# Top-32 attention and a PReLU feed-forward on one core: score products moved behind h, VectorE's order fixed, the norm after the searches, and half of the wide copies on VectorE

## The chip, the cores and the metric

The kernel runs on one core of one Trainium2 chip. The metric is the device time of one execution in microseconds (us); lower is better. The kernel before takes 896.75 us, the median of three runs (896.16 to 897.48).

A core has five engines with queues of their own: PE (TensorE, matrix products; its weight loads are listed as PEld), ACT (ScalarE), DVE (VectorE), POOL (GpSimd) and SP (SyncE, which here only issues DMAs). Each works through its own list in order and waits where an instruction needs what another engine has yet to deliver.

## What is computed

Eight batches of eight heads, 576 queries and keys each, head size 64. Of each row of scores only those that are not below the 32nd largest are kept; the heads' outputs, side by side, are the 4608 tokens of a feed-forward layer (512 to 2048 to 512) with a PReLU between.

```python
scores = scale * q @ k.T                     # per head, 576 x 576
kth = np.partition(scores, -32, axis=-1)[..., -32:-31]
attn = softmax(np.where(scores >= kth, scores, -1e9))
x = concat_heads(attn @ v)                   # 4608 x 512
h = x @ w_in                                 # 4608 x 2048
g = np.maximum(h, 0) + alpha * np.minimum(h, 0)
out = g @ w_out                              # 4608 x 512
```

## The kernel before, in words

**Duos and slots.** The work on the 64 heads is cut into 144 *duos*: a duo is two blocks of 128 query rows of one pair of heads, or (a *tail duo*, `"m"`) the last 64 rows of the heads of two pairs. Each batch has 18 duos, two of them tail duos. The kernel is one loop, written out at build time, of 148 *slots* (`for n in range(ND + 4)`), and in slot n several duos stand at different stages: n is searched, n+1 is copied out, n-2 is compared and its rows searched (`count`, `row`), n-4 is masked (`relu`), n-5 is exponentiated (`exp`), n-6 is multiplied with v (`av`), and the pair of duos that ended with n-7 is normalised in even slots (`norm`).

**The stages of a duo.** `st_qk`: PE writes the scores, 128 x 2 x 576 in fp32, into `ps_sc`, a tile of three PSUM banks that exists once. `st_exit`: ACT copies it to SBUF (`s_sb`, six buffers). `dve_slot`: VectorE takes the 8 largest of each of six groups of 96 columns per row (12 MAX8, which write `up` and `small`); in an odd slot, for both duos of the pair n-1, n, it folds these to a threshold (`bot`, `th`, `neg`, `n8`, and in `turn` the first column of `p`). `st_count`: ACT takes the sign of (threshold - score) with a sum (`sg`, `cs`). `st_y`: GpSimd multiplies scores by that sign (`y`). `row`: VectorE finds the 8 largest of each row of `y`, one row search (0 or 1) for each of the duo's two blocks. `pick_steps` (`eq_`, `pk_`, `kt_`): three small VectorE steps choose the exact 32nd value (`KT`). `st_relu`: ACT makes a mask (`r`), and GpSimd subtracts it from the scores. `st_exp`: ACT writes exp to `w`, and SP issues a transposing DMA to `wT`. `st_av`: PE multiplies with v into `xo`, one PSUM buffer for a pair of duos; 10 products, 20 in a tail duo. `norm_a`, `norm_b`: VectorE's reciprocal of the sums, and the product `x` (`xm` for tails), which frees `xo`; SP then transposes x to `xT`.

**The feed-forward part** is fed in between. `h_pe` issues the 8 products (16 for 128-token chunks) of one unit of h (`ph`), `h_dve` is VectorE's ReLU to `gT`, `o_pe` issues a quarter of an output tile (`pz`), `o_act` is ACT's copy to `o_sb`. `keep_warm` issues four idle products (`rest`) where there is no h or no pz.

**Preparation.** `prep_pe` transposes k and q of a head pair for a later batch by PE (`tps`): two units of width 512 and one narrow unit per pair. `prep_evac` copies them to `qkT`; the list `pend` is emptied at the end of the slot, and `on_dve` decides between VectorE and ACT: wide ones by VectorE before slot 17 and by ACT from then on, narrow ones by VectorE after slot 16. `ph`, `tps` and `rest` share two PSUM buffers (`ps_h`).

**What sets the order.** Every engine is wrapped in `Ordered`, whose calls keep program order (line 31, which is why nearly every row of the profile has L31). An exception are the VectorE steps that go through `sm`: they use columns of one PSUM tile, `small`, and `declare_no_dep` takes the order among them away but for true overlaps, so the scheduler may move them, and with them the searches between. In the built list of before, the first search of the next slot stands ahead of `turn` and of the last row search, and `eq_` stands in the odd slot ahead of the fold.

PE's list in a slot of before is: h(n) or idle products, pz if ready, transposes, score(n+2), attention (n-6), and pz or idle products. ACT's list is: two signs, exp, two masks, the score copy of n+1, then output and `qkT` copies. GpSimd's is: two products `y`, two subtractions, and a cast of v in most slots.

## Time and profile before

| | |
|---|---|
| median of three runs | 896.75 us |
| the profiled execution | 892.84 us, of which 891.1 us from the first to the last instruction (the span) |
| mean granted PE clock | 0.967 of full speed |
| score copies: first, 25th, 144th | at 9.6, 152.7 and 834.0 us |
| PE, VectorE, ACT, GpSimd busy | 752.6, 745.7, 774.9, 757.3 us |

A row of a group reads: line, engine, operation, output <- input (buffer numbers left out), shapes, x count, then busy time in us and the mean ns of one, then the idle time of the engine just before these instructions and what ended it. A row of the waits reads: engine and what it wanted to do <- engine and what it waited for: us in total, times, longest. A row of the timeline reads: start, length, engine, line, operation, output <- input, shapes, count, and in brackets the idle time before it. Operations of one engine overlap a little at their ends, so the distance of two starts can be shorter than the length given.

### The profile page before, as it was taken

The page shows a single profiled execution, that of the slowest core. Times are in us where ns is not written, and L with a number is a line of the kernel's source. Part 1 is how long each engine was busy: PE and PEld are TensorE (multiplying, and loading weights), DVE is VectorE, ACT ScalarE, POOL GpSimd, SP SyncE. Part 2 cuts the span into 40 slices and gives each one's busy share as a digit, 9 for nine tenths or more (in the row PEclk, how much of TensorE's full clock was granted, in tenths as well). Part 3 has the DMA queues.
Part 4 walks back from the last instruction along what each step waited for, and adds up shares of the span by engine and source line. Part 5 has one row for each costly group of instructions (what it writes and reads, how often), then busy time and mean ns, then how long its engine had stood idle before and what let it go on. Part 6 is the DMA issues. An engine that isn't in the chain of part 4 may idle for free.

```text
span 891.1 us, 17698 instructions
## 1 busy us (share of the span) xinstructions
PE 752.6 (84%) x5299; PEld 431.9 (48%) x5386; DVE 745.7 (84%) x3451; ACT 774.9 (87%) x1279; POOL 757.3 (85%) x708
## 2 busy tenths in 40 slices
PE   8785989888888888888888888888878898888887
PEld 5342444444545454455445454454544555445554
DVE  4999786898997989998988889989898878898842
ACT  4899787899999999999998999999999879998930
POOL 2899787888998999989998899989998878998950
PEclk9899997999999999999989999999999989999999
DMA  8698974355555545555545556555555554343351
GB/s 177 160 199 149 158 126 86 78 108 114 125 112 113 119 96 125 103 121 114 123 100 111 108 101 134 101 125 114 116 112 119 102 103 92 79 89 63 85 101 40
DMA packets 344167, 100.19 MB, mean 112 GB/s; under 512 B 338032, under 2 KB 338048, under 8 KB 344064
## 3 DMA queue, kind: packets, MB, share of 16 engines
q1 hardware_dynamic: 340992, 91.87, 51.0%
q0 software_dynamic: 1872, 6.82, 3.2%
q8 instruction: 44, 0.72, 0.3%
q14 instruction: 59, 0.48, 0.2%
q10 hardware_dynamic: 1200, 0.30, 0.2%
HBM read 36.71 MB, written 9.44 MB: 52 GB/s over the span
## 4 chain that ended last, share of the span: by engine, by line
ACT 30%; PE 28%; DVE 13%; issue 12%; POOL 8%; DMA 6%; SPq 1%; ACTq 0%; POOLq 0%
PE ps_sc L31 9%; ACT r L31 9%; ACT sg L31 9%; ACT s_sb L31 7%; PE ph L31 6%; PE pz L31 5%; PE xo L31 5%; POOL y L31 5%; DVE p L31 4%; ACT w L31 3%; POOL s_sb L31 3%; DMA wT<-w 3%; DVE small L31 3%; DVE gT L31 3%; DMA q_st<-in_q_dram 3%
## 5 line engine op out<-in xcount | busy, mean ns | idle before, releaser
L31 POOL TENSOR_TENSOR y<-s_sb,sg 128x576 f32<-128x576 f32 x288 | 362.3, 1279 | 95.4 <-ACT sg L31 93.5
L31 POOL TENSOR_TENSOR s_sb<-s_sb,r 128x576 f32<-128x576 f32 x288 | 362.1, 1278 | 6.1 <-ACT r L31 6.0
L31 PE MATMUL ps_sc<-qkT 64*128 64x512 f32 (+2 forms) x768 | 184.2, 576 | 110.1 <-ACT s_sb L31 109.4
L31 ACT ACTIVATE sg<-s_sb,p 128x576 bf16<-128x576 f32 x288 | 220.8, 769 | 53.2 <-DVE p L31 53.1
L31 DVE MAX8 up<-s_sb 128x8 f32<-128x96 f32 x864 | 211.3, 245 | 15.5 <-ACT s_sb L31 14.3
L31 DVE MAX8 p<-y 128x8 f32<-128x576 f32 x288 | 210.4, 750 | 3.9 <-POOL y L31 3.8
L31 DVE MAX8 small<-s_sb 128x8 f32<-128x96 f32 x864 | 211.9, 252 | 0.0
L31 ACT ACTIVATE r<-s_sb,KZ 128x576 bf16<-128x576 f32 x288 | 205.5, 762 | 5.7 <-DVE KZ L31 5.6
L31 ACT ACTIVATE w<-s_sb 128x1152 bf16<-128x1152 f32 x144 | 165.7, 1151 | 4.7 <-POOL s_sb L31 4.7
L31 DVE TENSOR_SCALAR gT<-ph 128x512 bf16<-128x512 f32 x144 | 99.0, 688 | 76.9 <-PE ph L31 76.8
L31 ACT COPY s_sb<-ps_sc 128x1152 f32<-128x1152 f32 x144 | 158.2, 1099 | 3.2 <-PE ps_sc L31 3.0
L31 PE MATMUL ph<-xT,w_in_b 128*128 128x256 bf16 (+1 forms) x1408 | 153.0, 257 | 0.1
L31 PE MATMUL pz<-w_out_b,gT 128*128 128x512 bf16 x546 | 145.4, 386 | 5.2 <-issue 3.1
L31 PEld LDWEIGHTS ps_sc<-qkT 64*128 64x128 f32 (+1 forms) x768 | 54.1, 170 | 168.8 <-ACT s_sb L31 143.0
L31 PE MATMUL xo<-v,wT 128*128 128x65 bf16 (+3 forms) x1600 | 128.4, 200 | 7.3 <-DMA wT<-w 7.3
L31 PEld LDWEIGHTS <-w_in_b 128*128 128x128 bf16 x1408 | 116.6, 99 | 32.3 <-issue 3.0
L31 PEld LDWEIGHTS <-wT 128*128 128x128 bf16 (+3 forms) x1600 | 98.7, 100 | 38.0 <-DMA wT<-w 8.6
L31 PEld LDWEIGHTS ps_sc<-kd,qkT 128*128 128x128 f32 x256 | 38.9, 192 | 99.2 <-issue 98.5
L31 PEld LDWEIGHTS <-gT 128*128 128x128 bf16 x576 | 57.2, 99 | 57.8 <-issue 6.8
L31 PE MATMUL ps_sc<-kd,qkT 128*128 128x128 f32 x256 | 63.8, 332 | 0.0
L31 PE MATMUL rest<-idle 128*128 128x512 bf16 x209 | 59.2, 402 | 2.1 <-DVE qkT L31 0.7
L31 ACT ACTIVATION_READ_ACCUMULATOR sg<-s_sb,p 128x1 f32 x288 | 54.6, 190 | 0.0
(57 smaller groups left out, 562.5 us busy)
## 6 DMA issues: line engine op xcount, KB each, us to landing
k_st<-in_k_dram SPq DMA_DIRECT2D x64, 128.0 KB, 2.8
v_st<-in_v_dram SPq DMA_DIRECT2D x64, 128.0 KB, 2.7
q_st<-in_q_dram SPq DMA_DIRECT2D x62, 128.0 KB, 2.8
out_dram<-o_sb SPq DMA_DIRECT2D x31, 256.0 KB, 2.4
w_st<-in_moe_w_out_dram POOLq DMA_DIRECT2D x4, 1024.0 KB, 6.2
wT<-w SPq DMA_TRANSPOSE x144, 3.5
w_in_b<-in_moe_w_in_dram POOLq DMA_DIRECT2D x4, 512.0 KB, 5.8
k_st<-in_k_dram SPq DMA_DIRECT2D x32, 32.0 KB, 2.5
```

The source lines that it names most:

```text
L31: return self.tc.keep_in_program_order(f(*a, **kw))
```

## The change

Four things are changed.

1. In the loop, `st_qk(n + 1)` is called right after `h_pe` (or the idle products) at the head of slot n, from slot 1 on, and the call of `st_qk(n + 2)` between the transposes and the attention products goes. PE's list becomes: h(n) or idle products, score(n+1), pz, transposes, attention (n-6), pz or idle products.
2. `Ordered` records each call. A step named in `small` is placed behind the last step that isn't (`anchor`), and the next one that isn't is placed behind all small ones since. VectorE's built list is then the program's: `turn` and the last row search stand ahead of the next slot's first search, and `eq_` stands in the even slot after the first search of `small`.
3. In even slots `norm_a` is called after `h_dve`, and `norm_b` between the row searches 0 and 1. Before, the reciprocal stood after the first six searches and x after the twelfth, both ahead of gT.
4. Wide `qkT` copies go to VectorE in even slots after slot 16 too. These are 24 of them, in slots 22 to 124; on ACT 24 fewer stand in the built list. They stand at the end of VectorE's even slot.

The lists of GpSimd and SP keep their order.

```diff
--- before.py
+++ after.py
@@ -23,14 +23,38 @@
 
     def __init__(self, tc, eng):
         self.tc, self.eng = tc, eng
+        self.anchor, self.loose, self.last, self.small = None, [], None, set()
 
     def __getattr__(self, name):
         f = getattr(self.eng, name)
 
         def call(*a, **kw):
-            return self.tc.keep_in_program_order(f(*a, **kw))
+            ins = self.tc.keep_in_program_order(f(*a, **kw))
+            self.settle()
+            self.last = ins.ins
+            return ins
 
         return call
+
+    def behind(self, ins, other):
+        self.tc.add_manual_dep(
+            ins, other.name,
+            mybir.DependencyInfo(mybir.DependencyClass.NoSync, mybir.DependencyReason.DATA),
+            reason="program order")
+
+    def settle(self):
+
+        if self.last is None:
+            return
+        if self.last.name in self.small:
+            if self.anchor is not None:
+                self.behind(self.last, self.anchor)
+            self.loose.append(self.last)
+        else:
+            for i in self.loose:
+                self.behind(self.last, i)
+            self.anchor, self.loose = self.last, []
+        self.last = None
 
 
 def fast_path(tc, q, k, v, moe_w_in, moe_w_out, moe_alpha, out, flag):
@@ -123,6 +147,7 @@
                     if hit(writes, r[1]) or hit(writes, r[2]) or hit(reads, r[2])]
             tc.declare_no_dep(ins.ins, group="small", keep=keep, reason="other columns")
             tc.add_to_no_dep_group("small", ins.ins)
+            DVE.small.add(ins.ins.name)
             recent.append((ins.ins, reads, writes))
             del recent[:-60]
 
@@ -305,14 +330,15 @@
                             sm(m, [], [(o, o + 8)])
                             if picks:
                                 picks.pop(0)()
-                    if norm and i == 0:
-                        norm_a(norm)
-                if norm:
-                    norm_b(norm)
                 if n % 2 == 0:
                     h_dve()
+                    if norm:
+                        norm_a(norm)
                     for d in rows:
                         row(d, 0)
+                    if norm:
+                        norm_b(norm)
+                    for d in rows:
                         row(d, 1)
                 else:
                     fold, negate, least, turn = threshold_steps(n // 2)
@@ -701,6 +727,8 @@
                     st_av(m)
             if not h_pe() and not end:
                 keep_warm()
+            if n and on(n + 1):
+                st_qk(n + 1)
             late = len(hq) > (9 if n < 118 else 4) and n % 2 == 0 or end
 
             for m in duos_at("count", n):
@@ -720,8 +748,6 @@
             run(n, "cast")
             run(n, "lin_out")
             run(n, "prep", 2 if n < 4 else 1)
-            if on(n + 2):
-                st_qk(n + 2)
             if not end:
                 for m in duos_at("av", n):
                     st_av(m)
@@ -737,7 +763,8 @@
                 late_o[0] = 0
             while pend:
                 short = len(pend[0][0].shape) == 3
-                on_dve = short and n > 16 or pend[0][0].shape[1] == 512 and n < 17
+                wide = pend[0][0].shape[1] == 512
+                on_dve = short and n > 16 or wide and (n < 17 or n % 2 == 0)
                 prep_evac(DVE.tensor_copy if on_dve else ACT.copy)
             if n == 1:
                 sm(DVE.tensor_copy(alpha_ps, aps), [], [(304, 320)])
```

## Prediction

> **What bounds the kernel now.** I read the page first (span, busy shares), then the busy time by stretch, then the waits of the long middle stretch, then that stretch's timeline engine by engine. The page:

> ```profile
> span 891.1 us, 17698 instructions
> ...
> PE 752.6 (84%) x5299; PEld 431.9 (48%) x5386; DVE 745.7 (84%) x3451; ACT 774.9 (87%) x1279; POOL 757.3 (85%) x708
> ```

> Four engines have nearly the same work, and none is full: an even load that loses time in handing over. The table of stretches (start:end, length, then busy time of PE, PEld, DVE, ACT, POOL, then granted clock) says where:

> ```profile
> 0.00:152.00 152.00, 122.92 (x682) 63.02 (x694) 119.37 (x559) 123.86 (x211) 116.95 (x136) 0.92 0.78 151
> 152.00:834.00 682.00, 585.66 (x4190) 339.61 (x4257) 602.17 (x2828) 628.58 (x1035) 616.84 (x553) 0.98 0.51 107
> ```

> The middle stretch runs from the score copy of duo 24 to that of duo 143: 119 slots, 682/119 = 5.73 us each, 11.46 a pair of slots. ACT is busy for 628.6 of it and waits for the rest. The waits of that stretch name the ring:

> ```profile
> PE ps_sc L31 <- ACT s_sb L31: 89.8, 81, 2.5
> POOL y L31 <- ACT sg L31: 63.3, 69, 4.1
> DVE gT L31 <- PE ph L31: 60.0, 82, 3.9
> ACT sg L31 <- DVE p L31: 47.3, 36, 4.4
> ```

> Read as a ring: PE waits for ACT's copy out of the one score tile, VectorE waits for PE's h, ACT waits for VectorE's threshold, GpSimd waits for ACT's sign. One turn of it, slots 70 and 71 of the timeline, in fences for ACT, PE, VectorE (DVE) and GpSimd (POOL) (start, length, engine, group, idle before it):

> ```profile
> 417.84 0.78 ACT L31 ACTIVATE sg<-s_sb,p 128x576 bf16<-128x576 f32 x1 [1.44 <-DVE p L31]
> ...
> 419.37 1.15 ACT L31 ACTIVATE w<-s_sb 128x1152 bf16<-128x1152 f32 x1
> ...
> 421.76 1.10 ACT L31 COPY s_sb<-ps_sc 128x1152 f32<-128x1152 f32 x1
> 422.76 0.58 ACT L31 COPY qkT<-tps 128x512 f32<-128x512 f32 x1
> 423.23 0.78 ACT L31 ACTIVATE sg<-s_sb,p 128x576 bf16<-128x576 f32 x1
> ...
> 429.13 0.77 ACT L31 ACTIVATE sg<-s_sb,p 128x576 bf16<-128x576 f32 x1
> ```

> ```profile
> 416.46 1.13 PE L31 MATMUL ps_sc<-qkT 64*128 64x512 f32 x4 [0.83 <-ACT s_sb L31]
> ...
> 417.93 1.62 PE L31 MATMUL xo<-v,wT 128*64 128x65 bf16 x20
> 419.71 1.03 PE L31 MATMUL pz<-w_out_b,gT 128*128 128x512 bf16 x4 [0.16 <-issue]
> 420.57 1.04 PE L31 MATMUL ph<-xT,w_in_b 128*128 128x256 bf16 x8
> 421.45 0.60 PE L31 MATMUL tps<-ident_f,k_st 128*128 128x128 f32 x4
> 422.91 1.13 PE L31 MATMUL ps_sc<-qkT 64*128 64x512 f32 x4 [0.86 <-ACT s_sb L31]
> ...
> 424.29 0.78 PE L31 MATMUL xo<-v,wT 128*128 128x65 bf16 x10
> ...
> 429.69 0.78 PE L31 MATMUL xo<-v,wT 128*128 128x65 bf16 x10
> ```

> ```profile
> 418.86 0.18 DVE L31 SCALAR_TENSOR_TENSOR pk<-small,p 128x36 f32<-128x36 f32 x1
> 418.96 0.25 DVE L31 MAX8 up<-s_sb 128x8 f32<-128x96 f32 x1
> ...
> 420.63 0.41 DVE L31 TENSOR_TENSOR xm<-xo,KZ 128x256 bf16<-128x256 f32 x1
> 421.65 0.69 DVE L31 TENSOR_SCALAR gT<-ph 128x512 bf16<-128x512 f32 x1 [0.61 <-PE ph L31]
> 422.25 1.41 DVE L31 MAX8 p<-y 128x8 f32<-128x576 f32 x2
> 423.58 0.24 DVE L31 MAX8 up<-s_sb 128x8 f32<-128x96 f32 x1
> ...
> 425.50 0.18 DVE L31 TENSOR_TENSOR small<-small,cs 128x36 f32<-128x36 f32 x1
> ...
> 426.95 0.69 DVE L31 TENSOR_SCALAR gT<-ph 128x512 bf16<-128x512 f32 x1 [0.55 <-PE ph L31]
> ...
> 428.79 0.24 DVE L31 MAX8 up<-s_sb 128x8 f32<-128x96 f32 x1
> 428.95 0.15 DVE L31 TENSOR_SCALAR p<-small 128x4 f32<-128x4 f32 x1
> ```

> ```profile
> 418.78 2.52 POOL L31 TENSOR_TENSOR y<-s_sb,sg 128x576 f32<-128x576 f32 x2 [1.20 <-ACT sg L31]
> ```

> PE's score product (416.46) starts when ACT has emptied the tile; the attention products, pz and h stand behind it, so h ends at 421.45 and VectorE's gT stands idle for 0.61, and for 0.55 in the next slot. VectorE then runs through to the threshold at 428.95, and at 429.13 ACT's sign follows it. The pair took 429.13 - 417.84 = 11.29. From the score copy's end to the threshold the path is product 1.5, attention 0.75 (1.6 in a tail duo), pz 1.0, h 0.9, and then VectorE.

> **The change part by part.**

> *Score product behind h.* No instruction is added; PE's order turns to h(n), score(n+1), pz, transposes, attention. h(n) no longer stands behind the wait for ACT, so it is ready before VectorE wants it: the 60.0 of gT waits and the 47.3 of ACT waits lose their cause. What is late next is the score tile itself. On time, score(n+1) takes 1.5 from the copy's end (422.91 to 424.3), and ACT copies that tile again 421.76 - 417.84 = 3.9 after its slot begins: 2.4 us of slack for PE. In front of it stands h, whose PSUM buffer comes free with a gT of the slot before, or with a transposed tile's copy; I cost that at nothing as long as the 2.4 hold. The transposes and wT's DMA are met one slot earlier: w ends at 420.5, its transposing DMA takes 3.5 (below), so wT is there at 424.0 and is used at 429.7, 5.7 later. Afterwards it is used behind the score product of 422.91, at 424.3 plus pz or transposes: 0.3 to 1.8 of margin while PE is on time, more when it is late.

> ```profile
> wT<-w SPq DMA_TRANSPOSE x144, 3.5
> ```

> *VectorE's order pinned.* The threshold (428.95) no longer has the next slot's first search (428.79, 0.16 earlier) before it, nor the small compare (425.50, about 0.1) in its slot, which moves to the even slot. The ring to ACT is 0.26 shorter; VectorE's sum is unchanged. The early search cost no wait here, and it can't any more.

> *Norm behind the searches.* The reciprocal comes behind gT, and x (0.41) behind the first row search. By distances of starts 12 searches take 1.92 (423.58 to 425.50), a small step 0.1 (418.86 to 418.96), gT 0.6 and a row search 0.67 (422.25 to 423.58 for two). So x ends later. In an even slot, from its first search: searches 1.92, four small steps 0.4, gT 0.6, row 0.67, x 0.41: 4.0, against 1.92 + 0.4 + 0.41 = 2.75 now. PE's next attention product waits for x, since xo has one buffer. Queued behind it: pz, h(n+1), score(n+2). From x: 0.75 + 1.0 + 0.9 + 1.45 = 4.1, so score(n+2) ends 8.1 after VectorE's slot began. ACT's slot begins at the threshold, a row search (0.67) before VectorE's; its next slot begins 4.92 later (417.84 to 422.76, without copies) and wants the tile 3.9 after that: 4.92 + 3.9 - 0.67 = 8.15. Just in time; 0.8 late after a tail duo. xT's DMA starts 1.3 later too, but its h comes two slots later, which covers it.

> *Half of the wide copies to VectorE.* 24 copies, slots 22 to 124:

> ```profile
> L31 ACT COPY qkT<-tps 128x512 f32<-128x512 f32 x52 | 30.2, 581 | 7.4 <-PE tps L31 7.4
> L31 DVE COPY qkT<-tps 128x512 f32<-128x512 f32 x12 | 8.0, 681 | 12.0 <-PE tps L31 12.0
> ```

> ACT loses 24 x 0.58 = 13.9 of busy time, 24 x 0.47 = 11.3 by the distance of starts (422.76 to 423.23); I take 11.5, near the lower one, since ACT's groups follow each other by starts. VectorE gains 24 x 0.68 = 16.3, or 14.4 at 0.6, a gT's distance; I take 14.6 for the same reason and keep both ends for the range. The copy stands at the even slot's end, where VectorE is ahead of ACT's score copy by about 0.4; beyond that it is on the path.

> *Sum, middle stretch.* ACT 628.6 - 11.5 = 617; VectorE 602.2 + 14.6 = 617; GpSimd 616.8 as before; PE 586. No engine can make it in under 617, 65 below now. Three engines at the same floor won't meet it: by pairs, VectorE's mean pair is 602.2/59.5 = 10.1, with a wide copy 10.7; GpSimd's is 616.8/59.5 = 10.4; ACT's is 9.84, with a wide copy left to it 10.3, with an output copy too 10.8. Of 18 slots, four pairs have wide copies (10.75, the dearest engine), four have the narrow one (10.4), one has none (10.1): 94.7. The score tile that comes 0.8 late behind each of two tail duos adds 0 to 1.5, transposed tiles that ACT waits for about as much; I add 1.6: 96.3, or 5.35 a slot, 637 for 119. That is 45 less than 682.

> *First stretch.* 152 stays within about 4 either way. For: 5.0 us of ACT's waits for the threshold lie there. Against: a stall at 88.5,

> ```profile
> 88.54 1.06 PE L31 MATMUL xo<-v,wT 128*128 128x65 bf16 x10 [4.51 <-DMA wT<-w]
> ```

> will now stand in front of a score product that today is already issued; its copy comes some 7 us later, most of which is lost today to a VectorE copy behind the same stall. I take -1. *Drain:* same order of pz and h, no saving, +1 for work left over.

> The profiled execution took 892.84 (891.1 span and 1.7 around it), 3.9 under the median 896.75 of the runs. 45 off the median: **852**.

> **The rivals.**

> *A, the wait moves into PE's ring through x.* x to x: attention 0.75, pz 1.0, h 0.9, score 1.45, pz 1.0, transposes 0.5, attention 0.75, pz 1.0, h 0.9 = 8.25, then gT, reciprocal, row, x 1.78: 10.0 a pair, 11.4 with a tail duo (20 products for 10, and 0.6 more of scores). For it: PE's own work, 586/59.5 = 9.85 a pair, leaves little. Against: many slots lack one pz. If ACT waits add up to 11.1 a pair, 59.5 x 11.1 = 660: 22 off, 875.

> *B, slower: the wait for x cools PE.* After an idle of 2.05 us, the next stretch ran at half clock (stretch, length, PE busy, clock):

> ```profile
> 443.50:445.50 2.00, 0.15 (x1) 1.00 0.50 96
> 445.50:447.00 1.50, 1.30 (x6) 1.00 0.51 96
> 447.00:449.00 2.00, 2.00 (x17) 0.54 0.00 0
> ```

> On time, PE would reach the even slot's attention product up to 2 us before x (score tile taken up 1 us before VectorE's slot begins, then 1.5 + 1.0 + 0.5, against 4.0). If each even slot held such a gap, A's 8.25 would be stretched: 8.25/c + 1.78 passes today's 11.46 where the mean clock of the middle stretch falls under c = 0.85 (0.98 now). At 0.8 the pair is 12.1, 720 for the stretch: +38, 935. Against: PE's work of 9.85 in 10.7 leaves 0.85 of idle a pair, so once it runs late the gap is short. [...]

> *C, the reordering does nothing.* Should the threshold still end ACT's waits (GpSimd's rows late instead of h), only ACT's copies are saved: 11.5, less the 0.6 a time on VectorE, which then is in the ring: 885 to 897, I take 890.

> *D, floor reached.* All waits go: 65 off, 832.

> **How the numbers follow.** Forecast (838 to 868) 0.62; A 0.16; B 0.09; C 0.07 (0.04 of it faster, 0.03 no change); D 0.06. Faster is then 0.62 + 0.16 + 0.04 + 0.06. Low end: 834, since the floor itself is reached at most by D. High end: A with both dear copy costs, 882. Left out: B, most of C, a bit of D, 0.2 in all. The runs before differ by 0.15%, so 0.2% is about what can be told from no change. Faster 0.88, same 0.03, slower 0.09.

> **What will show it.** Right: in the middle stretch, gT's wait for h from 60 to under 15, ACT's wait for p from 47 to under 20, ACT and GpSimd over 95% busy, slots of 5.35; ACT 24 wide copies fewer. A: a new wait of PE's attention products (or their weight loads) for VectorE's x, and ACT's score copy waiting for PE, over 20 us. B: a mean clock under 0.85 there. C: ACT's wait for p still above 40 with gT no longer waiting. The forecast is wrong in size if the wait of attention for wT, which no row of the middle stretch's longer waits shows today, passes some 10 us, or if the first stretch grows past 158.

## Result, and the profile after

The changed kernel takes 883.02 us (median of four runs, 880.58 to 885.65) against 896.62 for the kernel before: a ratio of 0.985, 95% interval 0.982 to 0.988. It is faster, as forecast, but by 13.6 us (1.5%) instead of 45, and 1 us above the range's high end of 882. The profiled execution took 883.55, its span is 881.3. In all ratios, executions more than 1.5% longer than the fastest of the same kernel are left out; the one profiled of copies_back was such a one, so only its other times are used.

The page of the changed kernel, span and engines:

```profile
span 881.3 us, 17690 instructions
...
PE 773.3 (88%) x5299; PEld 438.1 (50%) x5386; DVE 764.1 (87%) x3475; ACT 765.5 (87%) x1255; POOL 755.6 (86%) x708
```

ACT's work fell by 9.4 and VectorE's rose by 18.4, near the forecast. PE's rose by 20.7 with the same number of products. The stretches, cut at the 25th and the last score copy (161.9 and 822.0 now; columns as before):

```profile
0.00:162.00 162.00, 126.11 (x698) 64.06 (x710) 123.41 (x562) 124.26 (x212) 118.33 (x137) 0.91 0.70 142
162.00:822.00 660.00, 601.07 (x4172) 343.71 (x4238) 616.49 (x2849) 618.88 (x1010) 613.80 (x552) 0.95 0.55 110
822.00:881.30 59.30, 46.09 (x433) 30.33 (x440) 24.17 (x66) 22.34 (x36) 23.43 (x21) 0.93 0.32 74
```

The middle stretch is 660.1 long from copy to copy: 21 shorter, where 45 was forecast. The first is 9 longer (forecast -1), the last 2 longer (forecast +1). The waits of the middle stretch answer to the four rows shown of before, with the new ones between:

```profile
POOL y L32 <- ACT sg L32: 45.5, 52, 3.2
PE xo L32 <- DVE x L32: 43.3, 31, 2.8
ACT s_sb L32 <- PE ps_sc L32: 34.1, 25, 3.3
DVE gT L32 <- PE ph L32: 19.7, 22, 2.4
...
PE pz L32 <- ACT o_sb L32: 6.6, 8, 1.1
...
ACT sg L32 <- DVE p L32: 4.3, 10, 0.5
```

The old ring is gone: ACT's wait for the threshold fell from 47.3 to 4.3, VectorE's for h from 60.0 to 19.7, and PE no longer waits for ACT's score copy (89.8 before). In their place stands a new ring: PE waits 43 us for x, and ACT 34 us for the score tile. One turn of it, one of the longest, with PE, VectorE and ACT of the changed kernel (start, length, idle before); the score product in it is a tail duo's, which has 16 pieces:

```profile
461.58 0.22 PE L32 MATMUL tps<-ident_f,q_st 64*128 64x64 f32 x1
464.25 1.04 PE L32 MATMUL xo<-v,wT 128*128 128x65 bf16 x10 [2.44 <-DVE x L32]
465.22 0.61 PE L32 MATMUL pz<-w_lin_b,xT 128*128 128x512 bf16 x1
465.62 1.91 PE L32 MATMUL pz<-w_out_b,gT 128*128 128x512 bf16 x4
467.33 1.91 PE L32 MATMUL ph<-xT,w_in_b 128*128 128x128 bf16 x16
469.17 2.84 PE L32 MATMUL ps_sc<-qkT 64*64 64x512 f32 x16
```

```profile
463.70 0.40 DVE L32 TENSOR_TENSOR x<-xo,KZ 128x256 bf16<-128x256 f32 x1
...
469.28 0.69 DVE L32 TENSOR_SCALAR gT<-ph 128x512 bf16<-128x512 f32 x1 [1.59 <-PE ph L32]
...
473.27 0.26 DVE L32 MAX8 up<-s_sb 128x8 f32<-128x96 f32 x1 [1.19 <-ACT s_sb L32]
```

```profile
467.58 1.43 ACT L32 ACTIVATE r<-s_sb,KZ 128x576 bf16<-128x576 f32 x2
472.12 1.12 ACT L32 COPY s_sb<-ps_sc 128x1152 f32<-128x1152 f32 x1 [3.11 <-PE ps_sc L32]
```

PE is early at 461.8 and stands until x is written at 464.1. Then everything that is queued behind has to run first: attention, pz, h, and only then the score product that ACT would have taken at 469.0. It comes at 472.1. The pieces are also longer than usual (pz 1.91 for 1.03, h 1.91 for 1.06 at 459.01). The stretch table of PE shows why (stretch, length, PE busy, clock, then DMA share and GB/s):

```profile
460.00:462.00 2.00, 1.80 (x10) 1.00 0.62 137
462.00:464.00 2.00, 0.00 (x0) 0.94 0.24 48
464.00:466.00 2.00, 1.75 (x12) 0.50 0.96 180
466.00:468.00 2.00, 2.00 (x11) 0.50 0.35 70
468.00:470.00 2.00, 2.00 (x14) 0.50 0.53 155
470.00:472.00 2.00, 2.00 (x16) 0.86 0.82 153
```

The half clock began within the idle time, at 463.75, and lasted until 470.58. The mean over the middle stretch went from 0.98 to 0.95.

Two turns of the changed kernel with the same idle time show what the clock makes of it. Both times PE waited 2.17 us for x ahead of a tail duo's attention, and what stood behind was of about the same length: an output quarter or idle products, h, and an ordinary score product. PE's row and ACT's next score copy of each:

```profile
211.95 1.59 PE L32 MATMUL xo<-v,wT 128*64 128x65 bf16 x20 [2.17 <-DVE x L32]
...
312.23 1.64 PE L32 MATMUL xo<-v,wT 128*64 128x65 bf16 x20 [2.17 <-DVE x L32]
```

```profile
217.17 1.12 ACT L32 COPY s_sb<-ps_sc 128x1152 f32<-128x1152 f32 x1 [0.36 <-PE ps_sc L32]
...
318.82 1.12 ACT L32 COPY s_sb<-ps_sc 128x1152 f32<-128x1152 f32 x1 [1.73 <-PE ps_sc L32]
```

Behind the first the clock stayed at 1.00 and the score product ended 5.1 us after PE had x; behind the second it was 0.50 from 313.6 to 317.0, and the same took 6.5 us. It is so in the whole middle stretch: 14 of ACT's 25 waits for the score tile, 27.5 of the 34.1 us, end within a half-clock stretch or at most 6 us behind one, though these stretches with the 6 us behind them cover only 139 of the 660 us.

### The profile page after: what moved, and what is told of

The parts are those of the page before. It is cut to its first block, busy times and chain, and to the rows that moved or that the text cites. A ratio compares the mean times of both kernels' runs of the same rounds, so it can differ in the third digit from the quotient of the medians.

```text
span 881.3 us, 17690 instructions
## 1 busy us (share of the span) xinstructions
PE 773.3 (88%) x5299; PEld 438.1 (50%) x5386; DVE 764.1 (87%) x3475; ACT 765.5 (87%) x1255; POOL 755.6 (86%) x708
## 4 chain that ended last, share of the span: by engine, by line
PE 36%; DVE 29%; ACT 14%; POOL 10%; issue 5%; DMA 4%; SPq 1%; ACTq 0%; POOLq 0%
PE ps_sc L32 10%; PE pz L32 10%; DVE small L32 9%; DVE p L32 7%; PE ph L32 7%; DVE up L32 5%; PE xo L32 5%; POOL s_sb L32 5%; POOL y L32 4%; ACT sg L32 4%; ACT s_sb L32 4%; DVE gT L32 3%; PE rest L32 3%; ACT r L32 3%; ACT w L32 2%
## 5 line engine op out<-in xcount | busy, mean ns | idle before, releaser
L32 DVE MAX8 up<-s_sb 128x8 f32<-128x96 f32 x864 | 212.6, 246 | 18.9 <-ACT s_sb L32 18.4
L32 DVE MAX8 p<-y 128x8 f32<-128x576 f32 x288 | 215.2, 747 | 10.2 <-POOL y L32 9.7
L32 DVE MAX8 small<-s_sb 128x8 f32<-128x96 f32 x864 | 216.6, 251 | 0.0
L32 PE MATMUL ps_sc<-qkT 64*128 64x512 f32 (+2 forms) x768 | 186.1, 583 | 3.5 <-ACT s_sb L32 3.5
L32 PE MATMUL xo<-v,wT 128*128 128x65 bf16 (+3 forms) x1600 | 129.0, 201 | 67.7 <-DVE x L32 47.1
L32 PE MATMUL ph<-xT,w_in_b 128*128 128x256 bf16 (+1 forms) x1408 | 161.4, 265 | 0.9 <-PE xo L32 0.5
L32 PE MATMUL pz<-w_out_b,gT 128*128 128x512 bf16 x557 | 152.3, 396 | 5.6 <-issue 3.2
L32 PEld LDWEIGHTS <-w_in_b 128*128 128x128 bf16 x1408 | 121.5, 103 | 38.0 <-issue 9.5
L32 PE MATMUL rest<-idle 128*128 128x512 bf16 x209 | 62.7, 421 | 4.7 <-DVE qkT L32 2.7
```

The costliest lines, as they stand in the source:

```text
L32: ins = self.tc.keep_in_program_order(f(*a, **kw))
```

## The experiments

The table gives medians and ratios to the kernel before (with 95% intervals), and from each profile the middle stretch (score copy 25 to 144), its clock, and the three waits of the ring there in us ("-": not among the longest waits of that stretch). The profiled execution can lie some us off the median: that of no_idle took 856.9, that of head_old 879.9, that of score_only 879.9.

| kernel | us | ratio | middle, us | clock | PE for x | PE for output copy | ACT for score tile |
|---|---|---|---|---|---|---|---|
| before | 896.6 | 1 | 681.2 | 0.98 | - | - | - |
| changed | 883.0 | 0.985 (0.982 to 0.988) | 660.1 | 0.95 | 43.3 | 6.6 | 34.1 |
| norm_back | 873.7 | 0.977 (0.973 to 0.981) | 646.9 | 0.97 | 14.2 | 24.6 | 22.6 |
| norm_last | 901.4 | 1.006 (1.002 to 1.010) | 672.5 | 0.95 | 46.8 | 4.6 | 47.1 |
| pz_first | 894.3 | 0.995 (0.991 to 0.998) | 670.3 | 0.95 | 15.2 | 41.7 | 45.0 |
| skip_only | 877.8 | 0.979 (0.976 to 0.982) | 652.1 | 0.97 | 36.6 | - | 30.1 |
| pz_first_skip | 856.1 | 0.959 (0.953 to 0.964) | 629.6 | 0.99 | 12.6 | - | 11.2 |
| norm_back_skip | 851.6 | 0.953 (0.948 to 0.958) | 626.8 | 0.99 | 12.6 | - | 7.6 |
| no_idle | 851.4 | 0.948 (0.944 to 0.953) | 629.5 | 0.96 | 26.6 | - | 10.7 |
| score_only | 883.6 | 0.988 (0.983 to 0.993) | 660.0 | 0.97 | 8.8 | 37.7 | 21.8 |
| copies_back | 881.1 | 0.983 (0.980 to 0.987) | not used | | | | |
| free_order | 881.5 | 0.983 (0.979 to 0.986) | 660.1 | 0.96 | 41.5 | 9.2 | 31.6 |
| head_old | 875.5 | 0.978 (0.974 to 0.983) | 663.4 | 0.95 | 44.0 | 6.7 | 34.0 |
| v3 | 851.8 | 0.950 (0.947 to 0.954) | 629.7 | 0.99 | 13.4 | - | 7.6 |
| after_no_idle | 880.7 | 0.982 (0.976 to 0.988) | 659.2 | 0.95 | 53.4 | 9.9 | 33.5 |
| skip_no_idle | 872.3 | 0.972 (0.966 to 0.977) | 646.1 | 0.96 | 55.6 | - | 25.9 |

### x early and x later: norm_back and norm_last

norm_back takes one edit of the four back; norm_last goes further the other way.

```diff
# norm_back: against the changed kernel, in the searches and after them
+                    if norm and i == 0:
+                        norm_a(norm)
+                if norm:
+                    norm_b(norm)
                 if n % 2 == 0:
                     h_dve()
-                    if norm:
-                        norm_a(norm)
                     for d in rows:
                         row(d, 0)
-                    if norm:
-                        norm_b(norm)
-                    for d in rows:
                         row(d, 1)
# norm_last: norm_b(norm) behind row(d, 1) instead of behind row(d, 0)
```

> The changed kernel with the norm back among the searches (the reciprocal after six searches, x after twelve); the other three edits stay. Theory G (the gap): in even slots PE waits up to 2.8 us for x, its clock halves, and the score product behind runs late, 34 us of ACT's waits in the middle stretch. x some 1.3 us earlier shortens each gap below the 2 us that halve the clock: ACT's wait for the score tile in the middle stretch falls from 34 to under 12, the clock there rises from 0.95 to 0.98, and the time falls by 15 to 25, to about 863. Theory F (the floor): three engines with 614 to 619 of work each can't do better than the 660 of the middle stretch by any move of x; the time stays within 4 of 883. Theory O (the old order of the norm was there for a reason): the reciprocal waits for PE's attention inside the searches, so VectorE loses 10 or more and the time is over 890.

> The changed kernel with x behind both row searches of the even slot, 0.67 us later than now: a larger dose of the suspected wait. Theory G: PE's wait for x in the middle stretch goes from 43 to 65 to 85, more gaps pass 2 us, the clock falls to 0.93 or less and ACT's wait for the score tile rises from 34 to 45 to 60: 893 to 908. Theory F: within 5 of 883.

x earlier by 1.3 us gains 9 us, x later by 0.67 loses 18 (12 in the middle stretch, 8 in the first, 2 won back in the last), so x's place is a cause, with a dose. Theory G's way to norm_last's time was right only in part: ACT's wait for the score tile rose to 47.1 as expected, but PE's wait for x came to 46.8, not 65 to 85, and the clock stayed at 0.95. The 2 us of theory G is the author's estimate, from the gap of 2.05 us in the trace of before, behind which the clock was 0.50; no run shows a limit there (last section).

norm_back's gain is smaller than theory G expected (873.7, not 863; ACT's wait 22.6, not under 12); theories F and O, with times within 4 of 883 or over 890, fall. Its profile shows what holds the gain back: a wait that was 6.6 in the changed kernel. The row from norm_back's waits in its middle stretch, and one such place on PE:

```profile
PE pz L32 <- ACT o_sb L32: 24.6, 19, 2.2
```

```profile
577.08 0.78 PE L32 MATMUL xo<-v,wT 128*128 128x65 bf16 x10
579.89 0.38 PE L32 MATMUL pz<-w_lin_b,xT 128*128 128x512 bf16 x1 [2.03 <-ACT o_sb L32]
580.11 1.02 PE L32 MATMUL pz<-w_out_b,gT 128*128 128x512 bf16 x4
580.97 1.04 PE L32 MATMUL ph<-xT,w_in_b 128*128 128x256 bf16 x8
581.94 1.13 PE L32 MATMUL ps_sc<-qkT 64*128 64x512 f32 x4
```

The output quarter at the slot's end (`o_pe` after `o_act`) is the first of a new tile and needs the one output tile, which ACT copies out only after its score copy, at the end of its slot. Before the change the score product stood ahead of it and had waited for that same slot end, so the quarter found the tile free: no such wait is among those of before. With the score product at the slot's head, PE is there most of a slot earlier, and h and the next score product stand behind the wait.

### The gap filled, and the output tile: pz_first, norm_back_skip, pz_first_skip, skip_only

```diff
# skip (norm_back_skip, pz_first_skip, skip_only)
+                held = len(stores)
                 o_act()
+                freed = n > 24 and not end and len(stores) < held
...
-                if not (end or ready() > 2) or not o_pe():
+                if not (end or ready() > 2) or freed or not o_pe():
# pz_first (pz_first, pz_first_skip): in even slots after 26 the attention
# products come behind this output quarter or the idle products
+            swap = n > 26 and n % 2 == 0
-            if not end:
+            if not end and not swap:
                 for m in duos_at("av", n):
                     st_av(m)
...
                 late_o[0] = 0
+            if not end and swap:
+                for m in duos_at("av", n):
+                    st_av(m)
```

> The changed kernel, but from slot 28 on the last output quarter (or the idle products) of an even slot is put ahead of the attention products that wait for x, so that PE has 1.0 us of work in the gap; x stays late. Theory G: gaps of 2.0 to 2.8 become 1.0 to 1.8, the clock stays up (0.97 or more in the middle stretch), ACT's wait for the score tile falls from 34 to under 15, the time by 12 to 22, to about 866. Theory F: within 4 of 883. A theory that the wait itself, not the clock, costs the time also expects a gain, but one without a rise of the clock.

> The kernel with the norm back among the searches, and in a slot in which ACT's output copy is issued, from slot 25 on, idle products stand in place of the output quarter at the slot's end. Theory P (that quarter needs the one output tile, which ACT frees only at the end of its slot, and h and the score product stand behind it: 24.6 us of PE's waits in 19 places): PE's wait for the output copy falls under 6, ACT's wait for the score tile from 22.6 to under 10, the middle stretch from 647 to 635 to 640, the time from 873.7 to about 864. Rival F (the floor of three engines is what is left, the wait is hidden): within 3 of 873.7.

> The changed kernel (x late) with both: the output quarter of even slots ahead of attention, and none in a slot in which ACT's output copy is issued. Theories G and P together: the first kernel of this kind lost to the output tile (41.7 us of PE's waits for the copy) what it gained in the gap; without that, the gap ahead of attention is filled, the clock in the middle stretch is 0.97 or more, ACT waits under 20 for the score tile, and the time is 865 to 874. If the gap and the clock didn't matter, the time stays with the changed kernel's, 880 to 886.

> The changed kernel with one edit: in a slot in which ACT's output copy is issued, from slot 25 on, no output quarter stands at the slot's end, but idle products. x stays late, behind the first row search. Theory P2 (the late output quarter and the late x are two waits in one ring, each of which is dear because the other has used up PE's slack): without the quarter most of the loss goes although x stays, 858 to 868, with a clock of 0.97 or more in the middle stretch. Theory G alone (the wait for x is the cause): the quarter waited for only 6.6 us in the changed kernel, so 876 to 883, and the wait for x stays over 35.

pz_first missed both ways, at 894.3 where 866 or about 883 was expected: filling the gap with the output quarter only put that quarter's own wait (41.7) into it. With the quarter gone where the tile isn't free, the same filling gives 856.1 (865 to 874 was expected), though x is as late as in the changed kernel. norm_back_skip takes 851.6, 12 less than theory P expected, a ratio of 0.953 (0.948 to 0.958) to the kernel before and some 31 under the changed one; of all kernels only no_idle and v3, which are built on it, are level with it.

The two waits don't add: x alone is worth 9 (883.0 to 873.7), the quarter alone 5 (877.8), both 31. That they don't add is measured; why is not shown. Theory P2 explains it so: a wait is dear when the other has used up PE's slack. But P2 also expected 858 to 868 of skip_only, which took 877.8 with 36.6 us of waits for x, as theory G alone said, so the two waits aren't alike: x has to come early, or its gap be filled, before putting off the quarter pays.

The page of norm_back_skip and the waits of its middle stretch show what such a kernel looks like when the ring is open:

```profile
span 848.1 us, 17855 instructions
...
PE 770.6 (91%) x5376; PEld 435.5 (51%) x5466; DVE 759.9 (90%) x3475; ACT 763.3 (90%) x1255; POOL 754.3 (89%) x706
```

```profile
POOL y L32 <- ACT sg L32: 12.7, 23, 1.3
PE xo L32 <- DVE x L32: 12.6, 16, 1.7
...
ACT s_sb L32 <- PE ps_sc L32: 7.6, 12, 1.1
```

Its middle stretch is 626.8 with 616.6 of ACT's work in it. So the floor of 617 in the prediction's sum stands, and was met within 10 us.

### Is it the half clock? no_idle, after_no_idle, skip_no_idle

```diff
         def keep_warm():
+            if now[0] > 24:
+                return
```

> The best kernel so far (norm among the searches, no output quarter behind an output copy; 851.6) without idle products from slot 25 on: PE has some 30 groups of four fewer, 25 to 30 us of work, and no wait is added. Theory G in its strict form (the price of a gap is the half clock behind it): gaps that the idle products filled pass 2 us, the clock in the middle stretch falls from 0.99 to 0.96 or less, and the time rises by 6 to 20, to 858 to 872. Rival W (a gap costs only its own length): less work for PE, so the time is the same or lower, 846 to 853.

> The changed kernel without idle products from slot 25 on: x late, the output quarters where they are. PE has about 14 groups of idle products fewer there, some 12 to 15 us of work. Theory K (in the changed kernel, where PE has no time to spare, the half clock behind a gap is the price): the clock in the middle stretch falls below 0.95 and the time rises by 5 to 15, to 888 to 898. Theory W (PE's lost time is the price, whatever it comes from; the clock costs only what it adds to PE's work): less work, so 875 to 885.

> The changed kernel without an output quarter behind an output copy (877.8) and without idle products from slot 25 on, 25 to 30 us of PE work less; x stays late. Theory K: the clock falls from 0.97 to 0.94 or less and the time rises to 882 to 895. Theory W: 866 to 878, and the wait for x grows by about what the work shrinks.

Three kernels, each without the idle products from slot 25 on. The clock of the middle stretch fell in two of them (0.99 to 0.96, 0.97 to 0.96) and stayed at 0.95 in the third, and none became slower: 851.6 and 851.4, 877.8 and 872.3, 883.0 and 880.7. The last two without idle products ran on another chip than skip_only, so their ratios to the kernel before count: 0.972 against 0.979 and 0.982 against 0.985, with intervals that overlap, the first pair's just. That speaks against theories G (strict) and K, which expected all three to be slower.

It doesn't price the half clock by itself, since PE also has less to do in these kernels: in the middle stretch 575 us against 596, 578 against 608, 583 against 601. What is shown is that these idle products are worth nothing here. In the changed kernel the half clock does cost: PE's busy time in the middle stretch is 601 against 585 before, 16 us more for about as many products (4172 and 4190) at a mean clock of 0.95 against 0.98, and most of ACT's waits for the score tile come with it, as seen above. In no_idle, with x early and the quarter put off, a mean clock of 0.96 in the middle stretch goes with only 10.7 us of such waits, against 34.1 at the changed kernel's 0.95. The reading that fits all of these is theory W's: PE's lost time is the price, from whatever source, and the half clock is one source. A kernel with x late and the clock up, otherwise the changed one, wasn't tried, so the half clock's share isn't shown.

### The single edits: score_only, copies_back, free_order

score_only is the kernel before with edit 1 alone; copies_back and free_order are the changed kernel without edit 4 and without edit 2 (`self.settle()` and the line after it taken out).

```diff
# copies_back
-                on_dve = short and n > 16 or wide and (n < 17 or n % 2 == 0)
+                on_dve = short and n > 16 or wide and n < 17
```

> The kernel before with the move of the score products alone; VectorE's order loose, the norm among the searches, wide copies on ACT. Theory G: the move itself is worth nearly all of what was forecast, since x is early here: VectorE's wait for h in the middle stretch falls from 60 to under 20, and the time to about 870, under the changed kernel's 883. Theory F: between before and the changed kernel, 885 to 893, since ACT keeps 24 copies (11 us). Both expect the first 17 slots to be 10 to 15 us longer than before, because attention meets wT a slot earlier.

> The changed kernel with all wide copies after slot 16 on ACT again. Theory G: ACT's 11 us come back, but VectorE's 24 copies ahead of odd slots' thresholds go; where PE is late ACT waits anyway, so the time changes by less than 6 (877 to 889). Theory F (ACT, VectorE and GpSimd at one floor): ACT's work in the middle stretch goes from 619 to 630 and the time up by about 11, to 894.

> The changed kernel without the pinned order of VectorE (only the loose order among its small steps, as before). In the built order only the small compare moves, from the even slot to the odd one ahead of the threshold. All theories: within 5 of 883; a gain or a loss over 8 would mean that the pinning matters by itself.

Edit 1 alone gives 883.6, as much as the four give together. But that is two effects that cancel: norm_back, which is edits 1, 2 and 4, takes 873.7 (ratio 0.977, 0.973 to 0.981, against 0.988, 0.983 to 0.993), so edits 2 and 4 together are worth 10 us while the norm is early, and edit 3 takes 9 away. In the changed kernel, with the norm late, neither can be told: 881.1 with the copies back (theory F's 894 falls), 881.5 without the pinned order. There the work that the copies save is on an engine that waits for PE. Which of edits 2 and 4 brings the 10 us wasn't tried.

Theory G's 870 for edit 1 alone was missed; PE's wait for the output copy is 37.7 us in score_only, so the output quarter is the likely reason, but score_only without that quarter wasn't run. Its 18th score copy came at 119.9 instead of 107.6, 12 us later, as both theories expected.

### The first stretch: head_old and v3

head_old keeps the old place of the score products up to slot 23; v3 is norm_back_skip with the same.

```diff
-            if n and on(n + 1):
+            if n > 24 and on(n + 1):
                 st_qk(n + 1)
...
+            if n < 24:
+                st_qk(n + 2)
             if not end:
                 for m in duos_at("av", n):
```

> The changed kernel with the old place of the score products (behind the transposes, two duos ahead) up to slot 23 and the new one from slot 25 on. Theory H (the first stretch is lost because attention, and behind it the next score product, meets wT's DMA a slot earlier while the loads fill the DMA engines): the 25th score copy comes at 150 to 155 as before the change (161.9 in the changed kernel), the 18th at 107 to 110 (122.6), the middle stretch stays at 660, so 873 to 876. Rival L (other loads of the DMA engines from run to run, or the pinned order, make the difference): the 18th copy stays above 117 and the time at 880 or more.

> The best kernel so far with the old place of the score products up to slot 23 as well. If the losses add up as they were measured (8 in the first stretch, 23 from the output quarter, 9 from x), 843 to 848, against 851.6; if the first stretch's gain is given back later, 849 to 853.

In the changed kernel the 18th score copy comes at 122.6 instead of 107.6. One of the stalls, PE and ACT of the changed kernel:

```profile
57.36 1.07 PE L32 MATMUL xo<-v,wT 128*128 128x65 bf16 x10 [7.29 <-DMA wT<-w]
58.36 3.18 PE L32 MATMUL rest<-idle 128*128 128x512 bf16 x8
61.46 2.16 PE L32 MATMUL ps_sc<-qkT 64*64 64x512 f32 x16
```

```profile
63.73 1.12 ACT L32 COPY s_sb<-ps_sc 128x1152 f32<-128x1152 f32 x1 [4.42 <-PE ps_sc L32]
```

Attention meets wT too early, and the score product that used to be ahead of it is behind. Ahead of the 25th score copy the kernel before has one such stall, the 4.5 us of the prediction; the changed kernel has two, of 7.3 us (shown) and 8.6 (a weight load at 99.8), and none of the others passes 1.2. In the two long ones the DMA engines, with loads and transposing DMAs on them, showed a mean busy share of 1.01 (50.0 to 57.36 us) and 0.93 (91.2 to 99.8), against 0.70 over the stretch. With the old place there is one again, of 4.5 us, the 18th copy comes at 110.8, the 25th at 155.1, and the time is 875.5: theory H holds in the changed kernel. Added to the best kernel the old place brought nothing that can be told: 851.8 and 851.6. The stalls shrank there too, from 6.8, 4.3 and 2.0 us to one of 4.2, and the 18th copy came at 113.0 instead of 118.2, but by the 25th the lead was gone: 157.3 and 157.2. With the new place the 25th copy varied from 157.2 to 170.3 over the kernels profiled, and norm_back_skip's own profile has the 157.2. What takes the expected 4 to 8 us back in v3 stays open.

## Why the prediction was wrong, point by point

- **What bounds the kernel, and the ring.** Right. ACT's wait for p went to 4.3 (under 20 was named), and with the score move alone to 4.3 as well. gT's wait for h went to 19.7, not under 15. ACT and GpSimd came to 94% and 93% of the middle stretch, not over 95%, and a slot to 5.55 us, not 5.35.
- **The floor of 617.** Right: 618.9, 616.5 and 613.8 measured for ACT, VectorE and GpSimd, and 626.8 reached by norm_back_skip. The prediction's 637 for a kernel without a new ring was even too long, though norm_back_skip, with an early x and some output quarters put off, isn't the kernel it was meant for.
- **The step that failed: "Norm behind the searches", with its "Just in time".** The sum (x, then attention, pz, h and score, 8.1 against 8.15) was right at full clock: x was written 3.95 us after the slot's first search (460.15 to 464.10, 4.0 in the sum), and in the turn at 211.95 the score product ended 5.1 us after PE had x (4.1 and 0.8 for the tail duo in the sum). What failed, by the trace, is the full clock that it took for granted. Rival B named the gap of up to 2 us and the half clock behind it, but the forecast's sum has neither. At half clock the 5.1 became 6.5 in the turn at 312.23, and 7.8 in the turn shown first (464.25 to 472.01), whose score product is a tail duo's. The step was taken as no cost but for 0.8 behind tail duos, 1.6 in 18 slots or about 11 in the stretch, divided among late score tiles and transposed tiles; the late score tile alone measured 34.1. A sum that is just in time has no room for a slow piece, and here slow pieces stood behind some of the gaps that x makes (clock 0.50 behind those that ended at 312.23 and 464.25, 1.00 behind the one that ended at 211.95). That the late x costs is shown by norm_back, 13 us shorter in the middle stretch, and norm_last, 12 longer; that it does so by the half clock is read from the changed kernel's trace and not shown by a run of its own.
- **A step that was missing: the output quarter.** The prediction listed what is queued behind x, but did not ask what all the products that now come earlier would meet. Attention was checked against wT; the quarter behind it was not checked against the output tile. By itself this is 8 us of the middle stretch (skip_only), on top of an early x 20 (norm_back to norm_back_skip).
- **Half of the wide copies, VectorE's order.** Work moved as forecast (ACT 24 copies fewer); worth nothing in this kernel, not 11. With the norm early the two together bring 10 (score_only to norm_back).
- **First stretch.** The stall at wT was seen and priced at nothing ("most of which is lost today"); the forecast was -1, measured +9, and past the 158 that was named as a sign of being wrong (161.9). head_old shows the cause for the changed kernel. There were two long stalls, of 7.3 and 8.6 us, in place of one of 4.5. In the middle stretch, where the other sign was set, attention didn't wait for wT.
- **Rivals.** What happened is rival A, with a part of B: the wait moved into PE's ring through x (A's signs, both over 20 us, came to 43.3 and 34.1), and the clock was halved behind some of the gaps (0.50 from 313.6 and from 463.75). Its mean over the middle stretch stayed at 0.95, far above B's 0.85. A's middle stretch of 660 is what was measured (660.1), but that is partly luck: its 11.1 a pair was an assumption, it has no half clock and no output tile in it, and its 875 missed because the first stretch grew. Its 0.16 was too little for a ring that the prediction's own sum showed to be closed within 0.1 us.

In sum, for the profiled executions: 24 us of the forecast gain missing in the middle stretch (of them 13 for x), 10 in the first and 1 in the last.

## What to carry to other kernels

When a step is moved ahead on an in-order engine, everything behind it moves ahead too: ask of each of these what it will now meet early, since its wait holds the moved step's next turn: here an output tile (24.6 us of waits in norm_back), a DMA (7.3 and 8.6 us in the first stretch) and an operand (x, 43.3 us). A chain that comes out "just in time" is a closed ring, not a free one; price it by what one slow piece costs (here 5.1 us became 6.5). And waits in one ring needn't add: two that were worth 9 and 5 alone were worth 31 together here, so a removal that brings little isn't yet proof that the wait was harmless.

## What the runs showed of the hardware

```profile
200.00:400.00 200.00, 189.66 (x1349) 108.86 (x1370) 197.20 (x920) 198.17 (x326) 197.88 (x181) 0.99 0.63 123
```
